# Batch 1's Q and K transposed wholly by the DMA crossbar, with an earlier first request, a fuller start of the up projection, and one mask moved to VectorE

## The chip, the cores and the metric

The kernel runs on one core of a Trainium2 chip. The metric is the device time of one execution in microseconds (us), median of several runs; the kernel before takes 224.89 us (three runs, 224.43 to 225.37). Profiles are of one execution each, and their times count from the start of its span, which is some 1.7 us shorter than the measured time. "Clock" is the mean granted clock of TensorE over a run, 1.0 being full speed.

## The reference

Windowed causal attention with 4 sink tokens, then a two-layer feed-forward block with exact GELU:

```
q, k, v: float32 [4 batches, 8 heads, 768 positions, 64]
keep   = (key < 4) or (0 <= query - key < 128)
a      = softmax(where(keep, q k^T / 8, -1e9))
x      = (a v), heads side by side          -> [3072, 512]
out    = gelu(x w_in) w_out                 w_in [512, 2048], w_out [2048, 512]
```

## The kernel before

Batches are pipelined: while TensorE makes the down products of batch b (96 products of 128x128 by 128x512 in six blocks of 16), it takes up the attention of batch b+1 at fixed places between them. "Step n" below means "ahead of the down product number n". The schedule is manual: each engine's instructions stand in the order written, and in these traces one that waits holds up what stands behind it on its engine (experiment 5 shows VectorE standing for 3.87 us with ready work behind).

Q and K of two heads ("a pair"; four pairs in a batch) come as rows and have to be turned so that the 64 head dimensions lie along the partitions. There are two ways: six TensorE transposes with `ident` into PSUM, or one crossbar transfer on SyncE's DMA queue. Either is followed by `in_order`, a copy that reorders columns and writes `qkT`, the operand of the scores.

```python
def load_qk_casting(b, p, names=("q", "k")):      # GpSimd's queue, f32 -> bf16 on the way
    ...
        nc.gpsimd.dma_start(out=c, in_=rows_of(src, b, p))
def load_v(b, p, released_by=None):               # SyncE's queue
    ...
    nc.sync.dma_start(out=t, in_=v[b, 2*p : 2*p+2].rearrange("h (j s) d -> s h j d", s=P))
def heads_inside(b, p, ...):                      # VectorE regroups the rows of two heads
def transpose_on_pe(nm, b, p, engine): ...        # 6 TensorE transposes, then in_order on `engine`
def transpose_on_xbar(b, p): ...                  # q and k: nc.sync.dma_start_transpose
def order(b, p):                                  # in_order on VectorE of what the crossbar wrote
def cross(b, p):                                  # heads_inside, then transpose_on_xbar

        # ... batch 0's attention and three begun tiles of its up projection, cut ...
        for g in range(4):
            load_wout(g)                          # GpSimd's queue, casting
        for p in range(NPAIR):
            load_qk_casting(1, p)
        after(WOUT[2][0:1, 0, 0:2], 1)            # SyncE: a tiny copy that waits for WOUT 2
        load_v(1, 0)
        load_v(1, 1)
        # ...
        for p in range(2):
            heads_inside(1, p, spare=True)
        # down products of batch 0, with these steps of batch 1 between them:
                steps = batch_steps(1, 10) + [    # 10: the first scores of batch 1 are at step 10
                    (2, lambda: transpose_on_pe("q", 1, 0, nc.vector)),
                    (2, lambda: transpose_on_pe("k", 1, 0, nc.scalar)),
                    (8, lambda: transpose_on_pe("q", 1, 1, nc.vector)),
                    (8, lambda: transpose_on_pe("k", 1, 1, nc.vector)),
                    (9, lambda: cross(1, 2)),
                    (19, lambda: cross(1, 3)),
                    (20, late_values),
                    (31, lambda: order(1, 2)),
                    (40, lambda: order(1, 3)),
                ]
```

So before, pairs 0 and 1 of batch 1 go through TensorE and only pairs 2 and 3, which have time, through the crossbar.

The softmax here doesn't subtract the row's maximum and nothing guards it: scores larger than these inputs give would overflow.

## Time and profile before

| | before |
|---|---|
| time | 224.89 us |
| span of the profile | 223.3 us |
| TensorE busy | 213.5 us (96%) |
| first down product of batch 0 | 47.35 us |
| first scores of batch 1 (after 10 products) | 51.46 us |
| second scores of batch 1 (after 21 products) | 54.49 us |
| up projection of batch 1 starts | 78.30 us |

The stretch that the change works on is in the timeline of TensorE (columns: start in us, length, engine, line of the program, operation, output<-inputs, shapes, count, and in brackets the wait before it with what ended it):

```profile
47.35 0.38 PE L470 MATMUL ps_down<-WOUT,gt 128*128 128x512 bf16 x1
47.78 0.50 PE L248 MATMUL ps_tr<-ident,qP 128*128 128x128 bf16 x6
...
51.46 0.61 PE L302 MATMUL ps_big<-qkT 64*128 64x256 bf16 x8
52.01 2.55 PE L470 MATMUL ps_down<-WOUT,gt 128*128 128x512 bf16 x10
54.49 0.56 PE L302 MATMUL ps_big<-qkT 64*128 64x256 bf16 x8
```

Transposes and scores sit between the down products with one wait only, 0.36 us at 50.60. From the first down product to the first scores is 4.11 us, of which ten products take 2.16; so the 24 transposes with their waits cost 1.95. (The trace lacks some products: 10 shown where 11 were made.) A down product takes 0.216 us.

### The profile page before, as it was taken

What the parts mean: (1) busy time and instruction counts of PE and PEld (TensorE: products, weight loads), DVE (VectorE), ACT (ScalarE), POOL (GpSimd) and SP (SyncE); (2) the same over time, 40 slices, a digit from 0 to 9 for tenths busy, and PEclk for the clock granted to TensorE, in tenths of its full rate; (3) what the DMA queues carried; (4) which work ended last, traced back from release to release, by engine and by line L of the source; (5) the groups of instructions that cost most, each with busy time, mean ns of one, the idle gap of its engine ahead of it and who ended that gap; (6) DMA issues with size and microseconds to landing.
All of it is one profiled execution on the core that took longest, in us unless ns stands there. A gap on an engine that the chain in (4) does not pass through costs nothing.

```text
span 223.3 us, 4458 instructions
## 1 busy us (share of the span) xinstructions
PE 213.5 (96%) x1860; PEld 119.7 (54%) x1884; DVE 91.2 (41%) x183; ACT 118.3 (53%) x141; POOL 60.4 (27%) x85
## 2 busy tenths in 40 slices
PE   7789999999999999999999999999999999999994
PEld 2345655664555556554555556654555565654453
DVE  4466720038897410385757317404757200000010
ACT  4496456676555346669373346669473356551110
POOL 7749923333053456605144400000000000000000
PEclk9999999999999999999999999999999999999999
DMA  6999999999896999996799977300191810001212
GB/s 119 157 222 198 189 206 206 203 194 165 196 204 153 252 331 287 191 178 173 219 292 243 262 121 146 66 0 3 47 131 54 151 47 0 0 3 47 94 47 94
DMA packets 68055, 32.87 MB, mean 147 GB/s; under 512 B 52548, under 2 KB 65092, under 8 KB 68036
## 3 DMA queue, kind: packets, MB, share of 16 engines
q1 hardware_dynamic: 58004, 25.40, 52.5%
q0 software_dynamic: 10032, 7.20, 21.5%
q8 instruction: 14, 0.23, 0.4%
q14 instruction: 5, 0.04, 0.0%
HBM read 27.39 MB, written 6.29 MB: 151 GB/s over the span
## 4 chain that ended last, share of the span: by engine, by line
PE 85%; ACT 6%; DMA 3%; issue 3%; DVE 1%; POOL 1%; POOLq 0%; DVEq 0%; ACTq 0%
PE ps_big L437 36%; PE ps_down L470 34%; PE ps_av L358 6%; PE ps_big L302 5%; ACT et_t L322 3%; DMA c<-in_k_dram 3%; ACT gt L449 1%; PE ps_big L316 1%; PE ps_big L294 1%; PE ps_tr L386 1%; DVE x L367 1%; ACT L230 1%; PE ps_tr L253 1%; PE ps_down L437 0%; POOL c L100 0%
## 5 line engine op out<-in xcount | busy, mean ns | idle before, releaser
L470 PE MATMUL ps_down<-WOUT,gt 128*128 128x512 bf16 (+1 forms) x379 | 87.3, 370 | 1.2 <-issue 0.3
L437 PE MATMUL ps_big<-XT,WIN 128*128 128x384 bf16 x504 | 83.0, 326 | 0.2 <-ACT gt L449 0.2
L449 ACT ACTIVATE gt<-ps_big 128x768 bf16<-128x768 f32 x63 | 51.0, 811 | 41.8 <-PE ps_big L437 41.7
L437 PEld LDWEIGHTS <-WIN 128*128 128x128 bf16 x512 | 49.9, 98 | 33.4 <-issue 0.5
L322 ACT ACTIVATE et_t<-ps_big 128x1024 bf16<-128x1024 f32 x48 | 46.6, 1022 | 24.0 <-PE ps_big L302 21.4
L470 PEld LDWEIGHTS <-gt 128*128 128x128 bf16 x400 | 36.1, 98 | 35.4 <-issue 1.3
L114 DVE COPY osb<-ps_down 128x512 f32<-128x512 f32 (+1 forms) x12 | 8.0, 665 | 48.2 <-PE ps_down L470 48.2
L112 ACT COPY osb<-ps_down 128x512 f32<-128x512 f32 (+1 forms) x13 | 7.4, 572 | 30.0 <-PE ps_down L470 18.7
L114 POOL CAST c<-qk_f 128x768 bf16<-128x768 f32 x16 | 14.3, 897 | 27.4 <-DMA qk_f<-in_q_dram 21.9
L358 PEld LDWEIGHTS <-et_t 128*128 128x128 bf16 x480 | 18.0, 97 | 6.0 <-DVE x L367 0.3
L114 POOL CAST v<-v_f 128x768 bf16<-128x768 f32 x16 | 15.4, 963 | 20.1 <-DMA v_f<-in_v_dram 20.1
L328 DVE TENSOR_TENSOR et_t<-et_t,maskJ 128x1024 bf16<-128x1024 bf16 (+1 forms) x24 | 17.2, 720 | 7.4 <-ACT et_t L322 7.4
L358 PE MATMUL ps_av<-v,et_t 128*128 128x65 bf16 x352 | 18.3, 193 | 0.0
L367 DVE TENSOR_TENSOR x<-ps_av,rz 128x384 bf16<-128x384 f32 x32 | 17.8, 557 | 1.1
L302 PE MATMUL ps_big<-qkT 64*128 64x256 bf16 x192 | 15.2, 263 | 1.4 <-ACT qkT L112 0.4
L114 DVE COPY qkT<-qP 128x768 bf16<-128x768 bf16 x10 | 8.2, 821 | 20.0 <-DMA qP<-c 19.8
L328 DVE TENSOR_TENSOR et_t<-et_t,mask 128x1024 bf16<-128x1024 bf16 x12 | 9.0, 748 | 16.9 <-ACT et_t L322 16.9
L358 PE MATMUL ps_av<-vs,et_t 128*128 128x65 bf16 x128 | 14.5, 193 | 0.0
L302 PEld LDWEIGHTS <-qkT 64*128 64x128 bf16 x192 | 7.1, 94 | 12.4 <-issue 9.5
L114 DVE COPY qkT<-ps_tr 128x768 bf16<-128x768 bf16 x10 | 9.4, 956 | 8.0 <-PE ps_tr L253 4.6
L114 DVE COPY qkT<-kP 128x768 bf16<-128x768 bf16 x10 | 8.9, 886 | 2.5 <-DMA kP<-c 2.5
L136 POOL DMA_DIRECT2D vs<-in_v_dram x12 | 7.6, 640 | 1.9 <-DMA c<-in_k_dram 0.9
(59 smaller groups left out, 90.3 us busy)
## 6 DMA issues: line engine op xcount, KB each, us to landing
v_f<-in_v_dram SPq DMA_DIRECT2D x16, 384.0 KB, 6.3
out_dram<-osb SPq DMA_DIRECT2D x23, 256.0 KB, 2.5
qk_f<-in_q_dram SPq DMA_DIRECT2D x9, 384.0 KB, 3.6
qk_f<-in_k_dram SPq DMA_DIRECT2D x8, 384.0 KB, 4.6
WIN<-in_moe_w_in_dram POOLq DMA_DIRECT2D x4, 512.0 KB, 8.3
WOUT<-in_moe_w_out_dram POOLq DMA_DIRECT2D x4, 512.0 KB, 14.1
c<-in_k_dram POOLq DMA_DIRECT2D x8, 192.0 KB, 9.6
c<-in_q_dram POOLq DMA_DIRECT2D x7, 192.0 KB, 10.8
```

Source lines behind the costliest of these rows:

```text
L112: engine.copy(out=out, in_=in_)
L114: engine.tensor_copy(out=out, in_=in_)
L136: nc.gpsimd.dma_start(out=VST[b % 2][SKB * c : SKB * c + N_SINK, c, :, 0:D], in_=v[b, :, 0:N_SINK, :].rearrange("h s d -> s h d"),)
L230: nc.scalar.activation(out=warmed, in_=warm, func=AF.Exp)
L302: nc.tensor.matmul(ps[:, hl, col : col + nq * P], lhsT=kt[r : r + D, j, :], rhs=qt[r : r + D, j : j + nq, :].rearrange("d i s -> d (i s)") ...
L322: nc.scalar.activation(out=flat, in_=ps, func=AF.Exp, scale=att_scale)
L328: nc.vector.tensor_tensor(out=flat[:, :, 0:col], in0=flat[:, :, 0:col], in1=m.unsqueeze(1).to_broadcast((P, 2, col)), op=ALU.mult,)
L358: nc.tensor.matmul(pv[:, (i - half * n3) * 2 + hl, :], lhsT=lt, rhs=rh, start=(n == 0), stop=(n == len(parts) - 1),)
L367: nc.vector.tensor_tensor(out=self.x6[:, half * n3 : (half + 1) * n3, :, :].rearrange("s i h d -> s (i h) d"), in0=pv[:, :, 0:D], in1=rz.u ...
L437: nc.tensor.matmul(halves[hf], lhsT=WIN[f // 4][:, t, ts(f % 4, P)], rhs=XT[b, t][:, hf * HALF : (hf + 1) * HALF], start=(t == 0), stop=(t ...
L449: nc.scalar.activation(out=to, in_=whole, func=AF.Gelu)
L470: nc.tensor.matmul(po[:, 0:width], lhsT=GT[b, f][:, ts(m, P)], rhs=WOUT[f // 4][:, f % 4, c : c + width], start=(f == 0), stop=(f == NFT - 1),
```

## The change

It means to free TensorE of batch 1's 24 transposes and to shorten the start. Three parts:

1. **The start.** Pair 0's third score tile of batch 0 goes ahead of the second K's transposes; four tiles of the up projection are begun early instead of three; pair 2's first tile is masked by a VectorE product instead of two TensorE products.
2. **The crossbar.** All of batch 1's Q and K go through it; the first pair's load moves ahead of the last quarter of w_out.
3. **Places.** First scores at step 12, and others moved to suit.

Smaller moves go with the start (Q of batch 0's pair 3 is loaded ahead of V, two neighbouring calls change places). The diff is cut to its core; the kernel has the whole.

```diff
-            up_part(0, 1, (0, 1, 2))                 # ... part 1, cut to its core
-        a[3].turn()
-        up_part(0, 2, (0, 1, 2), apart=True)
+        up_part(0, 1, (2,))
+        up_apart(2, 0, ps_av())
+        a[3].turn()
+        up_apart(2, 1, ps_av())
+        up_apart(3, 0, ps_down())
+        up_apart(3, 1, ps_down())
-        score(a[2], "t0", "sum")
+        score(a[2], "t0")
-        for g in range(4):                           # ... part 2
+        for g in range(3):
             load_wout(g)
-        for p in range(NPAIR):
+        load_qk_casting(1, 0)
+        load_wout(3)
+        for p in range(1, NPAIR):
             load_qk_casting(1, p)
         after(WOUT[2][0:1, 0, 0:2], 1)
         load_v(1, 0)
-        load_v(1, 1)
-        for p in range(2):
-            heads_inside(1, p, spare=True)
+        heads_inside(1, 0, spare=True)
+        transpose_on_xbar(1, 0)
+        cross(1, 1)
-            up(b, begun=3 if b == 0 else 0)
+            up(b, begun=4 if b == 0 else 0)
-                steps = batch_steps(1, 10) + [       # ... part 3
-                    (2, lambda: transpose_on_pe("q", 1, 0, nc.vector)),
-                    (2, lambda: transpose_on_pe("k", 1, 0, nc.scalar)),
-                    (8, lambda: transpose_on_pe("q", 1, 1, nc.vector)),
-                    (8, lambda: transpose_on_pe("k", 1, 1, nc.vector)),
+                steps = batch_steps(1, 12, extra={1: 3, 4: 3}) + [
+                    (5, lambda: order(1, 0)),
                     (9, lambda: cross(1, 2)),
+                    (10, lambda: late_values(1)),
+                    (11, lambda: order(1, 1)),
                     (19, lambda: cross(1, 3)),
-                    (20, late_values),
-                    (31, lambda: order(1, 2)),
-                    (40, lambda: order(1, 3)),
+                    (22, lambda: late_values(2, 3)),
+                    (34, lambda: order(1, 2)),
+                    (46, lambda: order(1, 3)),
```

## The prediction

> **What bounds the kernel now.** I read the page's busy table first, then the chain that ended last, the waits of TensorE, the timeline around the first output product (40 to 62 us), and last the packet and completion records of the transfers.
>
> ```profile
> PE 213.5 (96%) x1860; PEld 119.7 (54%) x1884; DVE 91.2 (41%) x183; ACT 118.3 (53%) x141; POOL 60.4 (27%) x85
> ...
> DMA  6999999999896999996799977300191810001212
> ```
>
> TensorE is busy 96% of the span and the other engines about half or less, so only less TensorE work or shorter TensorE waits can gain. The second row (40 slices of 5.58 us) says that the transfer engines are full from about 6 to 50 us: until batch 1 is in, data arrives no sooner than the queues let it.
>
> ```profile
> PE ps_tr L253 <- DMA c<-in_k_dram: 1.2, 1, 1.2
> PE ps_big L294 <- ACT et_t L322: 0.4, 1, 0.4
> PE ps_big L302 <- ACT qkT L112: 0.4, 1, 0.4
> PE ps_tr L248 <- ACT qkT L112: 0.4, 1, 0.4
> ```
>
> These are TensorE's waits worth naming. The third is in the first scores and the change leaves it. The first (batch 0's second K, landing at 9.79) and the second (at 14.22) are what the first part attacks, the fourth (at 50.60) belongs to batch 1's transposes. From 55 us on TensorE has no wait that counts.
>
> ```profile
> 40.92 3.06 SPq L126 DMA_DIRECT2D v_f<-in_v_dram  x2
> 52.40 1.32 SPq L259 DMA_TRANSPOSE qP<-c  x1
> ...
> 53.09 1.30 POOL L114 CAST v<-v_f 128x768 bf16<-128x768 f32 x1 [4.95 <-DMA v_f<-in_v_dram]
> ```
>
> This decides the case. Batch 1's first V is asked for at 40.92 on SyncE's queue and its cast can start only at 53.09: the load took 12 us. In the completion records its sixteen shares land between 50.88 and 53.04; in the packet records SyncE's queue moves nothing from 40 to 44.5 us, then about 390 packets of 256 bytes in each 2 us beside some 390 of GpSimd's casting loads, one for one. This V is 1,536 such packets: 1,536/195 = 7.9 us after 44.5, or 52.4.
>
> **What the Trainium skill says.** (1) "DMA: Bandwidth & Descriptors", section "Queues, rings and completion order": SyncE's transfers share one row of rings, "on each SDMA engine descriptors are consumed in ring order", and each engine goes round-robin between queues that have work. The trace agrees: one for one above, and the crossbar transpose issued at 114.98, behind a V that lands at 120.54, completes at 121.14, while one issued at 67.88 with an empty queue took 3.3 us. (2) The same page, "Latency and other measured facts": two of the sixteen engines are usually slower. V's last two shares come at 53.02 and 53.04, the next before them at 52.49. (3) "TensorE: Matmul & The Clock Gate", "Part 1: The HAM clock gate": a whole idle window of about 3.4 us halves TensorE's clock, and it comes back only after about 3.4 us of work. In this trace the warm-up products of 512 columns start 0.427 us apart from 1.26 to 4.65; later ones keep 0.216.
>
> **The change part by part.**
>
> Start, batch 0. Pair 0's third score tile goes ahead of the second K's transposes, so it runs in the 1.19 us wait: its masks and scores, 0.32+0.33+0.18 = 0.8 us, are hidden. Pair 2's first tile loses its two 512-column mask products (2 x 0.216 = 0.43 us) and gains one VectorE product (0.75 us by the row of the same shape); VectorE then has qkT of pair 3 about 0.5 us later, just in time. Of these about 0.6 us survives at the first values, since the exponentials (1.0 us each) pace this stage. Four tiles begun instead of three put 6 x 0.163 = 0.98 us of work where TensorE waited for VectorE (0.5 to 0.7 us in all around 19.8, 23 and 25 us). The four shortened tiles then queue on ScalarE: pitches 0.70+0.70+0.88+0.88+0.81 = 3.97 us until a big buffer is free for the seventh tile, which TensorE reaches after 3.55: a wait of 0.4 in place of today's 0.25. Sum: the first output product starts near 46.3 instead of 47.35, **1.0 us gained**.
>
> Batch 1's transposes. 24 go, four groups of six at 0.34 us (six output transposes cost that in the chain at 76.40): 1.36 us, plus the wait of 0.36 and about 0.2 of gaps: **1.9 us**. Both gains together, 2.9 us, would be the end's if nothing waited.
>
> What the crossbar costs. The program order shows SyncE's queue as: gate behind the third WOUT, batch 1's first V, then Q and K of pairs 0, 1 and 2 by crossbar, then the second V. The first Q and K move up in GpSimd's queue: they land 0.98 us each behind the third WOUT (40.08), so near 41.1 and 42.1 instead of 43.60 and 44.59. But their crossbar transposes stand behind the first V on the same rings, and nothing about that V changes: same gate, same GpSimd traffic, the same wait to 44.5. So it is consumed at about 53 on the slow engines whether Q was early or not. Back-to-back crossbar transposes finish 0.7 to 1.2 us apart where they queue (92.81, 93.49, 94.68): Q near 53.8, K near 54.6. VectorE's reordering copies are 0.82 and 0.89 us: K is ready near 55.5. TensorE has 12 output products to do, 12 x 0.216 = 2.6 us from 46.3, and reaches the first scores at 48.9. Its stream is in order: **it stands for 6.6 us**, and the gains before that are swallowed.
>
> Balance at that point: before, the scores began at 51.46 after 10 products; now 55.5 after 12, so 55.5 - 51.46 - 0.43 = 3.6 us late. The rest follows as before: pair 1's Q and K land near 56.2, are reordered by 58.0, and are needed at 55.5+0.55+14 x 0.216 = 59.1. Masks that wait behind them may cost up to 0.5. That gives 224.9+3.6 = 228.5.
>
> Clock. An idle stretch of 6.6 us covers a full window of 3.4 with near certainty if the page holds here. Then 3.5 to 5 us of work runs at half speed: 1.7 to 2.5 us more, 230.2 to 231. I weigh it at about six in ten, so 1.1: **229.6**.
>
> **The rivals.**
> (a) The gain as intended. If the first V came early, or crossbar transposes overtook it, K would be ready near 48 to 49 and the sum is -2.9 plus 0.3 to 0.8 of small waits: 222.5. For it: the step numbers (reordering at step 5, scores at 12) suit data there by 48 us, so whoever set them expected it. Against it: the order of landings, which I found never reversed on this queue. About one in ten.
> (b) The stall without the slow clock: TensorE's idle window is not aligned, or the gate needs longer. 227.5 to 228.9.
> (c) The stall and the slow clock: 229.5 to 232. Together (b) and (c) hold nearly nine in ten.
> (d) GpSimd's K of pair 1 (47.28 before) as the limit: VectorE copies it inside before it reorders pair 0, so K of pair 0 is ready at the earliest near 49.4. A half microsecond at most; it matters only under (a).
> (e) VectorE as the bound: 41% busy, and the four removed evacuations offset the added copies. Not credible.
>
> **Range and chances.** The centre weighs (b) and (c). 226.3 allows V and K to arrive 2 us sooner without a slow clock, 232 a late K with it. Slower by over 2% means above 229.4: roughly the (c) half, 0.52. Faster by 2% means under 220.4, which not even (a) reaches: 0.02. The rest, 0.46, is within 2%.
>
> **What would show it.** In the changed profile: the first output product near 46.3 (else the start is mis-sized); no transposes of qP and kP on TensorE; one TensorE wait of 5 to 7 us before the first scores of batch 1, ended by VectorE's reordering, itself waiting for a crossbar transfer that lands at 53 to 55, just behind the V load; output products spaced 0.43 us after it if the clock fell; and from about 62 us on, the same pace as before. I am wrong if the crossbar result lands before 49 us, or if V lands clearly before 50: then ring order or sharing is not as I read it, and the time is near 222.5.

## More of the kernel before

The page of the kernel before, second and fourth parts: TensorE's granted clock in 40 slices (in tenths, 9 meaning 90% or more), and the shares of the chain of work that ended last.

```profile
PEclk9999999999999999999999999999999999999999
...
PE 85%; ACT 6%; DMA 3%; issue 3%; DVE 1%; POOL 1%; POOLq 0%; DVEq 0%; ACTq 0%
```

The clock is full in every slice, and the chain is TensorE's own work; transfers hold 3% of it.

## The result, and the profile after

The changed kernel takes **235.32 us** (four runs: 233.51, 234.61, 236.04, 236.62) against 225.13 us for the kernel before on the same chip (224.43 to 225.69): ratio 1.045, 95% interval 1.037 to 1.053. The four runs' clocks are 0.983, 0.978, 0.977 and 0.975: the shortest run has the highest clock. The profile is of that run.

The page after, the same parts as shown of before:

```profile
PE 215.7 (93%) x1858; PEld 118.7 (51%) x1858; DVE 91.0 (39%) x185; ACT 117.4 (51%) x141; POOL 59.5 (26%) x85
...
PEclk9999999995899999999999999999999999999998
...
PE 72%; DMA 13%; ACT 5%; DVE 4%; issue 3%; POOL 1%; ACTq 0%; DVEq 0%; POOLq 0%
```

TensorE is busy for 2.2 us longer although it has less to do, two slices in the middle have a clock of 5 and 8 tenths (the last slice, with 8, lies at the end of TensorE's work), and the share of transfers in the chain rose from 3% to 13%. The waits of TensorE (total, number, longest):

```profile
PE ps_big L303 <- DVE qkT L114: 8.6, 5, 6.1
...
PE ps_big L434 <- DMA XT<-x: 0.9, 1, 0.9
...
PE ps_tr L253 <- DMA c<-in_k_dram: 0.4, 1, 0.4
```

The wait at the start fell from 1.2 to 0.4 as intended, and a new one of 8.6 us stands at the top: 6.1 before the first scores, 1.2 in batch 0's start (experiment 1), 1.2 later. TensorE's timeline places the first and the last:

```profile
46.87 2.75 PE L482 MATMUL ps_down<-WOUT,gt 128*128 128x512 bf16 x12
55.74 1.03 PE L303 MATMUL ps_big<-qkT 64*128 64x256 bf16 x8 [6.12 <-DVE qkT L114]
56.70 4.76 PE L482 MATMUL ps_down<-WOUT,gt 128*128 128x512 bf16 x14
61.40 0.56 PE L303 MATMUL ps_big<-qkT 64*128 64x256 bf16 x8
...
69.45 0.61 PE L303 MATMUL ps_big<-qkT 64*128 64x256 bf16 x8 [0.84 <-DVE qkT L114]
```

After 12 products TensorE stands for 6.12 us. Then eight score products take 1.03 us, where before they took 0.61, and 14 down products take 4.76 us: 0.34 each, a mix of half and full speed. What TensorE waited for is VectorE's reordering, and VectorE's timeline says what that waited for:

```profile
54.16 0.81 DVE L114 COPY qkT<-qP 128x768 bf16<-128x768 bf16 x1 [6.69 <-DMA qP<-qP]
54.88 0.80 DVE L114 COPY qkT<-kP 128x768 bf16<-128x768 bf16 x1
```

The crossbar's Q landed at 54.14 and its K at 54.67 in the completion records. The issues on SyncE's queue show V in front of both transposes. The issues of these two took 6.64 and 3.02 us, where one at 55.98 took 1.21; what held them is not shown:

```profile
40.65 0.37 SPq L126 DMA_DIRECT2D v_f<-in_v_dram  x1
41.22 6.64 SPq L259 DMA_TRANSPOSE qP<-qP  x1
47.97 3.02 SPq L259 DMA_TRANSPOSE kP<-kP  x1
```

Last, what the stretches cost. The windows view gives length, then busy time of TensorE with its count, of the weight loads, VectorE, ScalarE and GpSimd, then clock, DMA share and GB/s:

```profile
46.87:55.74 8.87, 2.75 (x14) 1.08 (x13) 1.94 (x4) 2.30 (x3) 1.40 (x2) 0.85 1.27 189
55.74:61.40 5.66, 5.66 (x22) 2.11 (x23) 3.76 (x8) 2.52 (x3) 0.00 (x0) 0.63 0.64 134
61.40:86.00 24.60, 23.37 (x273) 12.88 (x273) 17.68 (x34) 12.04 (x13) 7.81 (x10) 1.00 0.93 190
```

In the first stretch TensorE worked 2.75 of 8.87 us; in the second it was busy throughout, but at 0.63 of its clock. The clock records give half speed from 53.09 to 59.92: 6.83 us, exactly two pieces of 3.413. TensorE worked in 4.18 of them (55.74 to 59.92), so half speed cost it 2.1 us.

The ledger of lateness against the kernel before, at equal work (a product more or less counts 0.216):

| at | before | after | late by | new in this stretch |
|---|---|---|---|---|
| first down product | 47.35 | 46.87 | -0.5 | start: gain 0.5 |
| first scores, 2 more products done | 51.46 | 55.74 | 3.85 | stall and gaps of 6.3, less 1.95 of transposes |
| second scores, 5 more products done | 54.49 | 61.40 | 5.8 | slow clock: 2.0 |
| up projection of batch 1 | 78.30 | 85.51 | 7.2 | later waits: 1.4 |
| end of the span | 223.3 | 231.8 | 8.5 | 0.9 of it a wait for an output transpose at 187.48 |

The last item is not explained here; in a second profile of the same kernel that wait was 1.1, and up to 0.7 in most others below.

### The profile page after: what moved, and what is told of

Its sections match the earlier page's. It is cut to its first block, busy times and chain, and to the rows that moved or that the text cites. A ratio compares the mean times of both kernels' runs of the same rounds, so it can differ in the third digit from the quotient of the medians.

```text
span 231.8 us, 4445 instructions
## 1 busy us (share of the span) xinstructions
PE 215.7 (93%) x1858; PEld 118.7 (51%) x1858; DVE 91.0 (39%) x185; ACT 117.4 (51%) x141; POOL 59.5 (26%) x85
## 4 chain that ended last, share of the span: by engine, by line
PE 72%; DMA 13%; ACT 5%; DVE 4%; issue 3%; POOL 1%; ACTq 0%; DVEq 0%; POOLq 0%
PE ps_down L482 30%; PE ps_big L434 28%; DMA c<-in_k_dram 6%; DMA qP<-qP 6%; PE ps_av L363 5%; PE ps_big L303 4%; ACT et_t L323 4%; DVE qkT L114 3%; DMA XT<-x 2%; POOL et_t L218 1%; PE ps_big L317 1%; PE ps_tr L391 1%; ACT gt L461 1%; PE ps_big L295 1%; PE ps_down L434 1%
## 5 line engine op out<-in xcount | busy, mean ns | idle before, releaser
L482 PE MATMUL ps_down<-WOUT,gt 128*128 128x512 bf16 (+1 forms) x400 | 92.3, 376 | 0.0
L434 PE MATMUL ps_big<-XT,WIN 128*128 128x384 bf16 x496 | 82.1, 326 | 1.1 <-DMA XT<-x 0.9
L461 ACT ACTIVATE gt<-ps_big 128x768 bf16<-128x768 f32 x62 | 50.1, 811 | 42.9 <-PE ps_big L434 42.9
L482 PEld LDWEIGHTS <-gt 128*128 128x128 bf16 x400 | 36.6, 99 | 37.2 <-issue 3.6
L114 POOL CAST v<-v_f 128x768 bf16<-128x768 f32 x16 | 14.3, 893 | 25.5 <-DMA v_f<-in_v_dram 25.5
L114 DVE COPY qkT<-qP 128x768 bf16<-128x768 bf16 x12 | 10.5, 874 | 23.6 <-DMA qP<-c 16.9
L329 DVE TENSOR_TENSOR et_t<-et_t,maskJ 128x1024 bf16<-128x1024 bf16 (+1 forms) x24 | 16.5, 689 | 7.4 <-ACT et_t L323 7.4
L329 DVE TENSOR_TENSOR et_t<-et_t,mask 128x1024 bf16<-128x1024 bf16 x13 | 10.1, 777 | 21.0 <-ACT et_t L323 21.0
L114 DVE COPY qkT<-kP 128x768 bf16<-128x768 bf16 x12 | 9.8, 816 | 6.7 <-DMA kP<-c 6.7
L114 DVE COPY qkT<-ps_tr 128x768 bf16<-128x768 bf16 x7 | 6.5, 951 | 4.1 <-PE ps_tr L253 3.2
```

Source lines behind the costliest of these rows:

```text
L114: engine.tensor_copy(out=out, in_=in_)
L329: nc.vector.tensor_tensor(out=flat[:, :, 0:col], in0=flat[:, :, 0:col], in1=m.unsqueeze(1).to_broadcast((P, 2, col)), op=ALU.mult,)
L434: nc.tensor.matmul(PH[f][0][hf], lhsT=WIN[f // 4][:, t, ts(f % 4, P)], rhs=XT[b, t][:, hf * HALF : (hf + 1) * HALF], start=(t == 0), stop= ...
L461: nc.scalar.activation(out=to, in_=whole, func=AF.Gelu)
L482: nc.tensor.matmul(po[:, 0:width], lhsT=GT[b, f][:, ts(m, P)], rhs=WOUT[f // 4][:, f % 4, c : c + width], start=(f == 0), stop=(f == NFT - 1),
```

## The experiments

All kernels below gave correct results. "Before" was run beside them each time, at 224.95 to 225.43 us.

### 1. The changed start alone

```diff
 # the changed kernel, with the loads, transposes and steps of the kernel before; begun=4 kept
-        for g in range(3): load_wout(g)
-        load_qk_casting(1, 0)
-        load_wout(3)
+        for g in range(4): load_wout(g)
-        steps = batch_steps(1, 12, extra={1: 3, 4: 3}) + [(5, order(1, 0)), ...
+        steps = batch_steps(1, 10) + [(2, transpose_on_pe("q", 1, 0, ...)), ...
```

> The changed start (third score tile ahead of K's transposes, pair 2's first mask on VectorE, four tiles begun) with batch 1 as in the kernel before. My sum says the first output product comes 0.5 (as in the changed kernel's profile, 46.87 against 47.35) to 1.0 us sooner, and nothing after it waits more: 224.1 to 224.7 us. Rival, that the start itself costs something later (VectorE's mask slows GpSimd, the ScalarE queue of four tiles): 225 us or more.

224.88 us (six runs) against 225.02 (eleven): ratio 0.999, interval 0.9974 to 1.0005. The profile, of the fastest run, has the first down product at 46.62 and every later landmark 0.73 us earlier than the profile of before. Across the runs that leaves 0.1 us in the median, and this profile is the luckiest: in the other profiles with the changed start the first down product comes between 46.63 and 47.38 (47.30 in experiment 8), with the old start at 47.35 and 47.84. The start gains 0.7 at most, hardly more than the scatter, and is no part of the loss. Why not 1.0 stands in TensorE's timeline of batch 0's first scores:

```profile
11.65 0.39 PE L303 MATMUL ps_big<-qkT 64*128 64x256 bf16 x4 [0.52 <-DVE qkT L114]
...
14.42 0.39 PE L303 MATMUL ps_big<-qkT 64*128 64x256 bf16 x4 [0.69 <-DVE qkT L114]
```

The wait of 1.19 for the second K went, and two waits for VectorE's reordering, 1.21 together, came a little later. The work slid forward to the next thing that was not ready. VectorE's new mask runs only at 15.91 in this profile, after both waits, so it is not what they waited for.

### 2. The crossbar part alone

```diff
 # the kernel before, with the loads, transposes and steps of the changed one; begun=3 kept
```

> Batch 1 by crossbar as in the change, the start as before. Theory: all of the loss is here, so K of pair 0 is ready near 55.5 whatever TensorE did earlier, the stall is about 0.5 us shorter than the changed kernel's 6.1 (TensorE arrives later), and the time is that of the changed kernel, 233 to 236 us. Rival, that half of the loss comes from the start's earlier arrival: 229 to 231 us.

235.11 us (233.72 to 235.95), ratio 1.044. The line of the stall in TensorE's timeline:

```profile
56.95 1.03 PE L302 MATMUL ps_big<-qkT 64*128 64x256 bf16 x8 [6.35 <-DVE qkT L114]
```

The whole loss belongs to the crossbar part, whatever the start. The stall is not the half microsecond shorter that I expected: K landed at 55.81 here, 1.1 us later than in the changed kernel.

### 3. V behind the transposes

My prediction said that V, standing in front in the ring, set the crossbar's time. This takes it away.

```diff
         after(WOUT[2][0:1, 0, 0:2], 1)
-        load_v(1, 0)
         ...
         cross(1, 1)
+        load_v(1, 0)
+        cast_v(1, 0, nc.gpsimd)
```

> The changed kernel with batch 1's first V issued behind the crossbar transposes of pairs 0 and 1. Theory as predicted (V is what stands in the ring): the queue then holds 768 packets for each transpose. If V alone is to blame, Q and K land near 45 and 46, K is reordered by 49.4, no stall worth naming, about 222.5 to 224. Theory refined by packets: SyncE's queue is served from 44.5 on and gets 195 packets a us beside GpSimd's casting loads until 52.9, so Q lands near 48.5 and K near 52.3, reordered by 53.2: a stall of about 3.7 us instead of 6.1, a shorter slow clock or none, about 229 to 231.

233.27 us (232.13 to 233.93), ratio 1.036. Its clocks are 0.982 to 0.984; the changed kernel's runs with such a clock took 233.51 and 233.65 (experiment 9), so hardly anything is gained. The stall is as long as ever:

```profile
55.91 1.03 PE L303 MATMUL ps_big<-qkT 64*128 64x256 bf16 x8 [6.12 <-DVE qkT L114]
```

K's transpose landed at 55.02 with nothing in front of it but Q's, and not near 52.3 as the packet rates had it. A second run of the same kernel, to see whether that was chance:

> The same kernel as the one with V behind, for a second profile, since the first had 2 us (50 to 52) in which both queues nearly stood. If that pause was chance, Q lands near 49.5 and K near 53.3 by the packet rates (195 a us from 45.5), and the stall is 4.4 us instead of 6.1; if transposes are simply slow beside casting loads, K lands at 55 again and the stall is 6.

234.75 us, a single run; the stall is 7.07 us, Q landed at 53.97 and K at 55.97. Packets per microsecond in that profile, by the queue they belong to (counted in the trace's packet records, one column for each microsecond):

```
us       46   47   48   49   50   51   52   53   54   55   56
GpSimd  207  194  195  186  116   29  318  124  143   27    0
SyncE   172  199  191  189  127   21  330  264  500  809  990
```

Up to 49 us the two queues move one for one, as in the profile of before, though now it is transposes and not V that share; when GpSimd's queue is empty SyncE's makes 800 to 1000. From 50.5 to 52 both nearly stood still, in this profile and in the first of this kernel, so this was not chance. So the claim that V in the ring was the cause is wrong. Two transposes are some 1,536 packets of 256 bytes, as many as V: whatever stands first in the ring gets half the packets while GpSimd's loads last, and much less than half the bytes, since GpSimd's packets from 45 to 50 us are nearly all of 768 bytes in the profiles of before and after. But sharing alone gave K near 52.3 and 53.3 by my estimates; the other 2.7 us in each profile are slow service from 50 us on, the near standstill among it, which is not explained.

### 4. TensorE kept busy through the stall

Zero products of 512 columns fill the wait, so that the clock cannot fall; all else is the changed kernel.

```diff
-                steps = batch_steps(1, 12, extra={1: 3, 4: 3}) + [
+                steps = [(12, lambda: busy(26))] + batch_steps(1, 12, extra={1: 3, 4: 3}) + [
```

> The changed kernel with 26 products of a zero tile (26 x 0.216 = 5.6 us) put into the stall before the first scores; the wait for K stays. If the slow clock after the stall is a cost of its own, the records show full clock throughout and the time falls by about 2.0 us (the 14 output products after the first scores take 3.0 instead of 4.7 us, the scores 0.5 instead of 1.0), to 231.5 in the state of the changed kernel's best run (233.5) and 233 of its median, with less scatter. If TensorE is in any case held by VectorE's masks and the later crossbar data, the time stays within 0.5 us.

231.59 us (230.66 to 232.38), ratio 1.029, clock 1.0 in the profile and 0.997 to 1.0 in all runs.

```profile
56.69 0.61 PE L303 MATMUL ps_big<-qkT 64*128 64x256 bf16 x8 [1.27 <-DVE qkT L114]
57.24 3.19 PE L482 MATMUL ps_down<-WOUT,gt 128*128 128x512 bf16 x14
```

The scores began no earlier than in the changed kernel, but the score products took 0.61 instead of 1.03 us and 14 down products 3.19 instead of 4.76. The changed kernel's runs with two pieces of half speed (233.51, and 233.65 in experiment 9) are 1.9 and 2.1 us longer than the median here: that is what the slow clock costs there. In the six profiles with a stall of 6 us or more before the first scores, half of the time worked at half speed is 1.5 to 2.6 us. The difference of the medians, 235.32 - 231.59 = 3.7 us, is an upper estimate: three of the changed kernel's four runs have a lower clock still, and these may also differ in the length of the stall, which no profile shows.

### 5. The later loads held back

If GpSimd's loads are the cause, taking them away must bring the first scores in time. GpSimd here copies two elements of pair 0's transposed K before it asks for Q and K of pairs 2 and 3 and the sink rows of V; so they are asked for once that K is there. Once with V behind the transposes, once with V ahead.

```diff
-        for p in range(1, NPAIR):
-            load_qk_casting(1, p)
+        load_qk_casting(1, 1)
         ...
+        heads_inside(1, 0, spare=True)
+        transpose_on_xbar(1, 0)
+        nc.gpsimd.tensor_copy(out=held, in_=PERM["k", 1, 0][0:1, 0, 0:2])
+        for p in range(2, NPAIR):
+            load_qk_casting(1, p)
         load_sinks_casting(1)
```

> V behind, and GpSimd's casting loads of pairs 2 and 3 held until K of pair 0 is through the crossbar. If the casting loads' share is what makes the crossbar late, SyncE's queue has the engines alone from about 47 on: K of pair 0 lands near 48.6, the first scores start near 50.2, the stall is 1 us or less and there is no slow clock; later waits for pairs 2 and 3 of 0 to 2 us; 224 to 227 us. If the crossbar is late for another reason, the stall stays over 3 us and the time over 229.

231.12 us (230.21 to 233.05), ratio 1.028: not the 224 to 227 expected. The timelines of TensorE, VectorE and GpSimd with V behind:

```profile
50.80 0.61 PE L304 MATMUL ps_big<-qkT 64*128 64x256 bf16 x8 [0.67 <-DVE qkT L114]
51.34 3.20 PE L483 MATMUL ps_down<-WOUT,gt 128*128 128x512 bf16 x14
58.41 0.80 PE L304 MATMUL ps_big<-qkT 64*128 64x256 bf16 x8 [3.87 <-DVE qkT L114]
```

```profile
54.61 0.97 DVE L175 COPY c<-c 128x768 bf16<-128x768 bf16 x1 [3.87 <-DMA c<-in_q_dram]
56.50 0.42 DVE L175 COPY c<-c 128x768 bf16<-128x768 bf16 x1 [0.92 <-DMA c<-in_k_dram]
56.85 0.79 DVE L114 COPY qkT<-qP 128x768 bf16<-128x768 bf16 x1
57.56 0.79 DVE L114 COPY qkT<-kP 128x768 bf16<-128x768 bf16 x1
```

The first scores are in time: 50.80 us, with a wait of 0.67, and earlier than in the kernel before. GpSimd's loads beside the transposes are shown to be the cause of the main stall (how much of it by the even share and how much by the standstill is not). But a new one took its place. VectorE stands at the regrouping of pair 2, whose held rows come at 54.52 and 56.41, and behind it in the program are the reordering of pair 1, in place since 51.23, and pair 0's masks. TensorE waits 3.87 us for pair 1, and half speed follows.

> The same hold, with V left ahead of the transposes as in the change. V's 1,536 packets then cost what they take: by the rates 507 go beside the casting loads until 47.1 and the rest at 1,000 a us until 48.2, so K of pair 0 lands near 49.8 and the first scores start near 51.6: a stall of 2 to 2.5 us, 1.2 to 1.6 more than with V behind, hardly a slow clock; 225 to 228 us. If V in the ring were the chief cause (my prediction), the stall stays near 5 to 6 us here while it vanishes with V behind.

230.86 us (230.51 to 231.27), ratio 1.026. With V ahead the first scores come at 52.05 after a wait of 2.45, and the second at 58.90 after 1.42. V in front puts K's landing from 49.91 to 51.07, some 1.2 us, once GpSimd's loads are out of the way; it is a part of the delay, and the smaller one. The stall is the 2 to 2.5 expected; the time is not the 225 to 228.

### 6. The held loads used later in the program

```diff
-                    (9, lambda: cross(1, 2)),
+                    (25, lambda: cross(1, 2, ("q",))),
+                    (28, lambda: cross(1, 2, ("k",))),
-                    (19, lambda: cross(1, 3)),
+                    (30, lambda: cross(1, 3)),
-                    (34, lambda: order(1, 2)),
-                    (46, lambda: order(1, 3)),
+                    (43, lambda: order(1, 2)),
+                    (53, lambda: order(1, 3)),      # V of pairs 2 and 3 from step 22 to 31
```

> As the kernel with V behind and the later pairs' casting loads held (231.12 us), but VectorE's regrouping of pairs 2 and 3, their crossbar transposes, their reordering and V of pairs 2 and 3 are moved later in the program order (step 9 becomes 25 and 28, 19 becomes 30, 34 becomes 43, 46 becomes 53). My theory: in that kernel the first scores came on time (50.80 us), and the loss had moved to VectorE's program order: it stood at the regrouping of pair 2, whose held load landed at 54.5 and 56.4, with pair 1's K in place since 51.2; so TensorE waited 3.87 us at 58.41 for pair 1, and the clock fell. Then here the second scores come at 54.5 to 55.5 without a wait over 0.5, no half clock is recorded, the waits for reordering sum to under 2 us, and the time is 223.5 to 226. If instead the crossbar transposes themselves are too slow whatever runs beside them (rival), a wait of over 2 us stays at one of the first three score groups and the time stays over 228.

230.58 us (229.54 to 230.84), ratio 1.022. The second scores came at 54.05 without a wait, as expected; the time did not follow. TensorE's waits:

```profile
PE ps_big L304 <- DVE qkT L114: 3.2, 4, 1.3
PE ps_av L364 <- DMA vs<-in_v_dram: 2.6, 1, 2.6
```

The sink rows of V, last of the held loads, came at 60.56, and the value products stood for them; half speed came again, from 61.35. It is not the main part of the loss: two of the four runs had a clock of 1.0 and still took 229.54 and 230.56. Asking for the sink rows ahead of the hold, and pair 3's reordering at step 44:

> As held_late (230.58 us), where the second scores came at 54.05 without a wait but three new costs were seen: 2.6 us at the value products for V's sink rows, whose casting loads had been held with the rest and landed last; one half-speed window of 3.41 us after it (1.7 us); and 1.26 us for pair 3's reordering, placed at step 53. Here the sink rows are loaded ahead of the hold and pair 3's reordering goes to step 44. If the rest of the loss is those three, they vanish, the sink rows put 0.5 to 1.5 us in front of the transposes (wait at the first scores 1 to 2.5 instead of 0.78), and the time is 225 to 227.5. If the wait only changes its name once more and the time stays at 229 or above, the held loads as a whole come too late for batch 1, whichever is last (rival).

229.10 us (228.08 to 230.98), ratio 1.014: better by the median, with overlapping runs, and still over the 225 to 227.5 expected. The profile is of the slowest run; in it TensorE waits 1.81 us at 64.80 for the reordering of pair 2, whose transposes had landed at 61.50.

### 7. The reordering copies placed earlier

Two kernels with only places changed: the changed kernel itself, and the last one.

```diff
 # the changed kernel
-                    (34, lambda: order(1, 2)),
-                    (46, lambda: order(1, 3)),
+                    (25, lambda: order(1, 2)),
+                    (40, lambda: order(1, 3)),
 # the kernel with held loads and early sink rows
-                    (43, lambda: order(1, 2)),
+                    (33, lambda: order(1, 2)),
```

> The changed kernel with nothing but the reordering of pairs 2 and 3 placed earlier in the program (step 34 becomes 25, 46 becomes 40). In its profile VectorE stood idle for 3.24 us from 59.65 to 62.89 while pair 2's K had been in place since 60.06, and reordered it only at 67.22; TensorE then waited 0.84 and 0.39 us. If those later waits are a matter of the order of VectorE's program, they vanish, the up projection of batch 1 starts near 84.3 instead of 85.51 in a profile with two half-speed windows, and the median falls by 1.2 from 235.3 (231.8 to 235.5, by the number of windows). If they come from the transfers, the waits stay.

232.82 us (232.53 to 233.17), ratio 1.033. The changed kernel's VectorE timeline held the reason:

```profile
62.89 1.01 DVE L329 TENSOR_TENSOR et_t<-et_t,mask 128x1024 bf16<-128x1024 bf16 x1 [3.24 <-ACT et_t L323]
...
67.22 1.47 DVE L114 COPY qkT<-qP 128x768 bf16<-128x768 bf16 x1
68.61 0.79 DVE L114 COPY qkT<-kP 128x768 bf16<-128x768 bf16 x1
```

VectorE stood for 3.24 us at a mask while pair 2's K was in place from 60.06, and reordered it only at 68.61. With the earlier place the third and fourth waits are gone:

```profile
69.38 0.61 PE L303 MATMUL ps_big<-qkT 64*128 64x256 bf16 x8
```

The main stall is still there (6.27 us), so is half speed for 6.83 us, and the up projection of batch 1 starts at 84.98. These two waits were a matter of where the copies stood in VectorE's program. At a like clock (0.985) the runs take 232.53 to 233.05, against 233.51 and 233.65 of the changed kernel: 0.5 to 1.1 us, a little under the 1.2 expected. The median fell by 2.5, which is more than the copies account for: only one of these four runs has a clock under 0.98, and three of the changed kernel's.

> As held_sinks_first (229.10 us), with the reordering of pair 2 at step 33 instead of 43. In that profile TensorE waited 1.81 us at 64.80 for it, though the transfer had landed at 61.5, and the clock then fell for two windows. If placement is what is left, the wait falls to under 0.7, at most one half-speed window is recorded, and the time is 225 to 227.5. If it stays at 228.5 or above, with a wait somewhere else over 1.5 us, then holding the loads costs batch 1 as much as it spares, wherever the copies are placed.

228.37 us (227.47 to 229.22), ratio 1.012 (again overlapping the runs of the version before), and the wait at the third scores is gone. What is left in the profile is a wait of 2.04 us at the first scores, one piece of half speed (3.41 us), a wait of 0.7 at the values and one of 0.5 for an output transpose. The one run with a clock of 1.0 took 227.47. The median falls between the two cases that I had named (225 to 227.5, and 228.5 or above), so placement was a part and not the rest.

### 8. One pair by TensorE, one by crossbar

```diff
 # the changed start alone (experiment 1)
-        load_v(1, 0)
-        load_v(1, 1)
-        for p in range(2):
-            heads_inside(1, p, spare=True)
+        heads_inside(1, 0, spare=True)
+        cross(1, 1)
+        for p in range(2):
+            load_v(1, p)
+            cast_v(1, p, nc.gpsimd)
-                    (8, lambda: transpose_on_pe("q", 1, 1, nc.vector)),
-                    (8, lambda: transpose_on_pe("k", 1, 1, nc.vector)),
+                    (11, lambda: order(1, 1)),
```

> The changed start alone (224.88 us) with pair 0 of batch 1 transposed on TensorE as before, pair 1 by crossbar (transposes issued as soon as its rows are regrouped, near 46.5 and 48), V of pairs 0 and 1 asked for behind them, nothing held. Theory of the one-for-one share: 1536 packets at about 195 per us from 46.5 to the end of the casting loads near 52.9 make some 1250, the rest lands by about 53.5, the reordering of K ends near 54.5, which is when the second scores are due (53.8 in the start alone, less 0.7 for twelve transposes gone): a wait of 0.5 to 2 us there, and 224 to 226.5 us. If the wait is over 3 us (K of pair 1 later than 55), the share is worse than one for one or something else stops the crossbar; if none at all and 223.5 to 224.3, then a crossbar transpose for one pair is free, and only the first pair was the mistake.

225.14 us (225.08 to 225.69), ratio 1.000, interval 0.998 to 1.002. K of pair 1 landed at 53.95, near the time expected, though on another road: SyncE's queue moved eight packets in all until 50 us, when GpSimd's was nearly through. The line of the second scores:

```profile
55.20 0.56 PE L303 MATMUL ps_big<-qkT 64*128 64x256 bf16 x8 [1.56 <-DVE qkT L114]
```

Twelve transposes are spared and a wait of 1.56 us is paid. Counted from the first down product, the second scores come 0.77 us later than in the start alone, so the twelve are worth about 0.8; in the times of the runs nothing is gained and nothing lost.

### 9. The mask on TensorE again, and a second profile of the change

```diff
 # the changed start alone
-        score(a[2], "t0")
+        score(a[2], "t0", "sum")
```

> The changed start with batch 1 as before, but pair 2's first tile masked by a product on TensorE again (0.43 us of TensorE work back, 0.75 us of VectorE work gone). If the mask on VectorE is a gain, this is 0.2 to 0.4 us slower than 224.88; if it costs as much as it gains (VectorE's mask delays the copies of pair 3, GpSimd's cast beside it takes 1.24 instead of 0.81 us), it is the same within 0.2 us or faster.

225.15 us (six runs), ratio 1.001 against before, interval 0.998 to 1.004: the mask's place is worth no more than 0.3 us, which these runs do not resolve.

> The changed kernel itself, a second profile. The first was of its fastest run (233.51 us, clock 0.983, two half-speed windows of 3.41 us); three other runs had clocks of 0.975 to 0.978 and 234.61 to 236.62. If those have a third half-speed window (10.24 us), a profile with a clock under 0.980 shows a half-speed record of 10.2 us and a span of 232.9 to 235; one with a clock over 0.982 shows 6.83 us. If a low clock comes with 6.83 us at half speed, the scatter has another cause.

233.65 us, clock 0.985, half speed for 6.83 us. It was again a run of the higher clock, so three pieces of half speed in the runs with 0.975 to 0.978 were not seen directly. They are inferred: two pieces go with 0.982 to 0.985 in every profile, one with 0.991 to 0.993, and a third takes off 3.41 x 0.5 / 233 = 0.007 more. Of the 18 runs of the four kernels whose profiles show a stall of 6 us or more (this one, experiments 2 and 3, the first of 7), 13 have a clock of 0.982 to 0.985 and five 0.975 to 0.978: two pieces are the usual case.

### When the clock fell

The clock records put every change on a grid of 3.413 us, with another phase in each profile. With TensorE's busy share in each piece of the grid, from the windows view of sixteen profiles, without the last pieces of the span:

| piece | busy share of TensorE | next piece |
|---|---|---|
| full speed | 0.00, 0.05, 0.09, 0.28, 0.31, 0.40, 0.47, 0.50 | half speed (in each of these profiles) |
| full speed | 0.53, 0.54, 0.56, 0.58, 0.61 and more | full speed |
| half speed | 0.00, 0.22, 0.40, 0.53, 0.54, 0.78 | half speed |
| half speed | 0.89, 0.93 and more | full speed |

The columns are as above, of TensorE alone. Two examples, of the kernel with held loads and V ahead, whose wait was 2.45 us, and of the kernel with early sink rows:

```profile
49.25:52.67 3.42, 0.97 (x11) 1.00 0.64 136
52.67:56.09 3.42, 3.42 (x9) 0.50 1.01 136
```

```profile
60.65:64.06 3.41, 1.71 (x17) 1.00 0.76 170
64.06:67.47 3.41, 2.67 (x13) 0.50 1.56 306
67.47:70.89 3.42, 3.20 (x24) 0.50 0.59 102
```

A piece that was half empty was enough for the clock to fall, and one that was 78% busy at half speed was not enough to raise it. So what one stall of 6.1 us costs depends on how it lies on the grid, which differs from profile to profile: 1.5 to 2.6 us in the six profiles.

## Why the prediction was right or wrong

The time, 235.32 us, lies above the range (226.3 to 232.0), with 229.6 as the centre. The chain of events was the one foretold: no transposes left on TensorE, a stall before the first scores ended by VectorE's reordering behind a crossbar transfer, then half speed. Step by step:

- **Start, 1.0 us gained.** Too large. The first down product came at 46.87 and 46.84 in the two profiles of the changed kernel, at 46.62 to 47.38 in all profiles with this start, so 0 to 0.7 was gained; in the medians of the start alone 0.1 is left. The missing part is the 1.21 us of new waits for VectorE's copies in batch 0, which TensorE now reached too early; they come before VectorE's mask, which I had charged with half a microsecond.
- **Transposes, 1.9 us gained.** Right: 1.95 in the profile before, and about 0.8 for half of them in experiment 8.
- **Q near 53.8, K near 54.6, ready near 55.5, TensorE stands for 6.6.** Right: 54.14, 54.67, 55.7 and 6.12. The lateness foretold at this point was 3.6; it measured 3.85. But the agreement is no proof of the cause: experiment 3 has K as late without V in front.
- **"But their crossbar transposes stand behind the first V on the same rings".** True, and not the cause that I made of it. With V out of the way K still came at 55.0 and 56.0. What delayed it is GpSimd's loads, which take every second packet from whatever SyncE's queue holds; a near standstill after 50 us, unexplained, came on top. Rival (a) fails by the same run: transposes ahead of V did not make K ready near 48 to 49. I had the one-for-one share on the table and used it for V alone, without asking what it does to the transposes if V goes.
- **"The rest follows as before", and "from about 62 us on, the same pace as before".** This step failed, and it is the largest miss in the profiled run: 2.7 us more were lost after the second scores, where the sum has nothing ("masks that wait behind them may cost up to 0.5" did not enter it). 1.4 came up to the next up projection, most of it TensorE's waits for the reordering of pairs 2 and 3 (0.84 and 0.39), which stood too late in VectorE's program, as experiment 7 shows. 1.3 came at the end, 0.9 of it one wait for an output transpose; its cause stays open.
- **"I weigh it at about six in ten, so 1.1".** The second step that failed, in the odds and not in the mechanism. The slow clock came in every one of those 18 runs (none has a clock over 0.985), and cost 2.0 in the profiled run, inside the 1.7 to 2.5 of my full case. Rival (b), the stall without it, could not happen by the table above: a stall of 6.1 us must leave some piece of 3.41 at least half empty, and half empty was enough. Odds of one would still have given 230.2 to 231, inside my range; it is the 2.7 above that goes beyond.

Summed with the measured terms from the profile: -0.5, then 3.85 + 0.5 = 4.35 to the first scores, 2.0 for the clock, 1.4 for the later waits, 1.3 at the end, gives 8.5, the difference of the two spans. Against my 229.6 the profiled run is 0.25 later at the first scores, 0.9 more for the clock and 2.7 for the rest: 233.45, and it took 233.51. The median run took 1.8 us more than the profiled one; a third piece of half speed would add at most 1.7, and its lower clock agrees, but no profile shows it.

"A time near 222.5 if the crossbar result lands before 49" was never reached: even with K of pair 0 in place at 49.5 to 50.5, the held loads, and the places of what uses them, cost the rest of the batch as much as was spared. The best kernel with all pairs by crossbar took 228.37 us. No version beat the kernel before: the start alone (224.88) and the half and half version (225.14) tie with it. Still open are the near standstill of both queues from 50.5 to 52 us in some profiles and the waits of 0.3 to 1.1 us for a later batch's transposed output.

## What to carry to other kernels

A transfer that replaces work on the bounding engine has to be priced at the rate that its queue gets in that stretch, with everything that shares the engines counted, not only what stands ahead in its own ring; and holding the other loads back moves the wait to those who need them, unless the order of every engine's program is changed with it. When a stall on TensorE is in the estimate, price the slow clock with certainty and not by odds when, as in these runs, a piece of 3.4 us will be half empty, and expect the cost to vary from run to run with the stall's phase. Write a term for what comes after the first stall, too: here it was 2.7 of 8.5 us. Before a copy is placed in the program, ask what else stands behind it while it waits.

## What the Trainium skill lacked or had wrong

- "TensorE: Matmul & The Clock Gate", "Part 1: The HAM clock gate", has the clock fall after an idle window and gives no busy share at which it does. The runs show it falling after windows in which TensorE was busy up to 0.50 of the time (1.71 of 3.41 us), and staying after 0.53 and more. Waits of 2.04 and 2.45 us were enough.
- The same section has the clock return after one busy window. The runs show that the window has to be nearly full: 0.89 and more sufficed, 0.78 did not, so that half speed lasted 6.83 us where work was resumed inside a window. The window of 3413 ns and its free running are confirmed: all changes lie on that grid.
- "DMA: Bandwidth & Descriptors", "Queues, rings and completion order", states turns between queues by packet, and the runs agree (188 to 199 packets a microsecond on each side from 45 to 50 us in the changed kernel). It does not say what this does to a crossbar transpose: beside casting loads, Q and K of one pair (128x768 bf16 each, some 1,536 packets of 256 bytes) took from 46 to 54 and 56 us (a near standstill of 1.5 us included, which stays unexplained), where SyncE's queue alone moves 800 to 1,000 such packets in one microsecond.
- The same page has no case of a queue that starts late beside another one's loads: V, asked for at 40.65 in the changed kernel, moved its first packets at 43.9, and the transpose of the half and half version, asked for at 47.43, at 49.96 (eight small packets before). With an empty queue later in the same profiles, a transpose's first packets come 0.4 to 1.2 us after its issue. Why they start late is not shown.
